# A pool for the score tiles that closes early, and the second stage's first weights decoded in it

## The chip, the cores and the metric

The kernel runs on one core of a Trainium2 chip. The metric is the device time of one execution in microseconds (us), as the median of several runs. Each core has a matrix engine (TensorE, in the rows PE, its weight loads PEld), three engines that work element by element (VectorE, DVE; ScalarE, ACT; GpSimd, POOL) and a queue that issues transfers (SyncE, SP). ACT issues transfers too, which then stand in its own queue (ACTq). Each engine works through its own instructions in the order of the program and waits, where it must, for a semaphore of another.

## The reference

Three parts follow each other. A recurrence over 768 steps for 4 x 8 heads of width 48, then two expert layers over the 3072 tokens of width 384:

```
cur   = (u * k_t) outer v_t
y_t   = r_t . (state + cur)
state = w_t * state + k_t outer v_t                      # 768 steps

x1 = (sigmoid(y @ w_gate) * (y @ w_val)) @ w_out         # 384 -> 1536 -> 384
h  = x1 @ w_in                                           # 384 -> 2048
out = (h * tanh(softplus(h))) @ w_out2                   # 2048 -> 384
```

## The kernel before

**Blocks.** Tokens are taken in 12 blocks of 64 steps for all batches, which are 256 tokens. For each block the recurrence runs in two steps of 32 (`step(j)`, 24 of them). Inside a block, the scores of eight steps and below are computed by POOL products (`pt`, from the block `blk` of r, k and w) and DVE sums into the tile `A`; larger distances go through PE (`lp`), and both are merged into `X`. PE makes the rows `yp`, ACT and DVE split them into two f16 halves `xs` (`split`, lines 202 and 205), and from block 2 on two transposing transfers that ACT issues (`send`, line 712) put them into `xt`, which the gates read. The state `s` is decayed (`decay`, line 754, on POOL or DVE) and joined with PE's outer products `kp` (line 792).

**First layer.** For block p, `gate(p, f)` with f = 0 to 11 makes two groups of 9 matmuls into one of four PSUM banks (`gv`, line 826), ACT takes the sigmoid (line 837), DVE multiplies (842), ACT and DVE write the f16 halves `gt` (854 and 857). `out1(p - 1, c, part)` runs beside it: for each of three columns c four groups of 9 matmuls into the single bank `po` (line 890), then ACT and DVE split the result into `xo` (202 and 205) and SP stores it. The next column's first group needs the bank back, and so the DVE half of `xo`.

**Second layer.** `h_unit` (PE at line 1006, weights `wis`) and `out2` (line 1051, weights `wps`) begin behind the last gate. Their 16 matmul groups per 512 tokens keep PE to the end.

**Weights.** All weights arrive as 64-bit numbers and are decoded in chunks to two f16 halves: `load_raw` (SP, 768 KB into a place `raw0` to `raw4`), on ACT `rebase` into `word` and `bits3` into `low`, on DVE `join` (line 273) and `sign` (284), then `high`, the cast (295, ACT or DVE), and `rest`, the subtraction (298, POOL or DVE). There are two `word` and two `low` places. `wi` has eight chunks and `wp` eight.

**Memory.** The recurrence's tiles lie in one pool `ap` on the right. `open_b` closes it when every task of the recurrence is done, and opens pools for `wis`, `wps`, two more `raw` places, two PSUM banks and the second layer's tiles in its room. So `high` and `rest` of `wi` and `wp` wait for `open`.

**Order.** The kernel does not write its order by hand: every piece is a task with an engine, an assumed cost, what it reads and what it writes, and `Plan.run` lays the tasks out in time by these costs and latest dates. The instructions are then issued in that order on each engine. A task that may run on two engines is put where it is planned first.

Of the kernel before, what the change touches and what calls it, by code (L numbers as in the profile page):

```python
# [7 lines left out]
F32 = mybir.dt.float32  # L8
F16 = mybir.dt.float16
# [7 lines left out]
DH = D // 2  # L17
# [6 lines left out]
BLK = C * (DH + DP + DH)  # L24
DM = H * D
KC = DM // 128
F1 = 1536
F2 = 2048
# [9 lines left out]
NPT = 32  # L38
NRAW = 2
# [8 lines left out]
W2HI = {"act": 0.83, "dve": 0.7}  # L48
W2LO = {"pool": 1.65, "dve": 0.92}
# [102 lines left out]
def mixer_moe_kernel(  # L152
# [23 lines left out]
    pg = ctx.enter_context(tc.tile_pool(name="pg", bufs=1, space=PS))  # L176
    po = ctx.enter_context(tc.tile_pool(name="po", bufs=1, space=PS))
    sa = ExitStack()
    sb = ExitStack()
    ap = sa.enter_context(tc.tile_pool(name="ap", bufs=1, side="right"))  # L180
    pp = sa.enter_context(tc.tile_pool(name="pp", bufs=1, space=PS, side="right"))

    x2d = dram.tile([NP, KC, 128, 2, NT], F16, name="x2d")
# [1 line left out]
    wgs = w1p.tile([128, 2, KC, F1], F16, name="wgs")  # L185
    wvs = w1p.tile([128, 2, KC, F1], F16, name="wvs")
    wos = w1p.tile([128, 2, NF1, DM], F16, name="wos")
    A = ap.tile([128, 1184], F32, name="A")
    KT = ap.tile([128, 2, BH, DP], F32, name="KT")
    U = ap.tile([128, DH], F32, name="U")  # L190
    mask = ap.tile([128, 2, C], F32, name="mask")
# [21 lines left out]
    def in_cols(w, s):  # L213
        v = w.bitcast(U32).rearrange("(c p) (f t) -> p c f t", p=128, t=2)
        return v[:, :, s]

    def in_rows(w, s):
        v = w.bitcast(U32).rearrange("(k p) (d t) -> p k d t", p=128, t=2)
        return v[:, s]
# [20 lines left out]
    def decode(key, dst, n, count, slot, reads, high_on, lo_on):  # L240
# [58 lines left out]
                out=dst()[:, 1], in0=words.pop(key), in1=dst()[:, 0], op=ALU.subtract  # L299
            )  # L300

        full = 1.55 if count < 6 else 0.95
        add("act", 0.9, rebase, [raw, "consts", "table1"], [word])
        add("act", 1.0, bits3, [raw, "consts"], [low])
        add("dve", full, join, [low], [word])
# [84 lines left out]
    blk = {}  # L390
# [21 lines left out]
    def load_pair(p):  # L412
        edges = (0, C * DH, C * (DH + DP), BLK)

        def new(e):
            blk[p] = ap.tile([128, BLK], F32, tag=f"blk{p % 2}", name=f"blk{p}")

        def go(e, i):
            if i is None:
                new(e)  # L420
            cs = slice(0, BLK) if i is None else slice(edges[i], edges[i + 1])
            nc.sync.dma_start(out=blk[p][:, cs], in_=rkw[p, :, cs])

        keys = [("blk", p % 2, i) for i in range(3)]
        if p:
            attn("sp", 3.6, lambda e: go(e, None), [], keys, lat=2.0)
        else:
            attn("none", 0, new, [], keys, lat=0.0)
            for i in range(3):
                attn("sp", 1.2, lambda e, i=i: go(e, i), [], [keys[i]], lat=2.0)  # L430
# [24 lines left out]
    def fine(p):  # L455
# [4 lines left out]
        def products(mult, cost, shape, cell, scaled=False):  # L460
            n = npt[0]
            npt[0] += 1
            pt = ("pt", n % 5)

            def go(e):
                pts[n] = ap.tile([128, NPT * DH], F32, tag=f"pt{n % 5}", name="pt")
                mult(e, shape(pts[n]), *rows(p)[:2])

            def times_u(e):
                u = U.unsqueeze(1).to_broadcast([128, C, DH])  # L470
                times(e, shape(pts[n]), shape(pts[n]), u)

            def total(e):
                nc.vector.tensor_reduce(  # L474
                    out=cell(), in_=shape(pts.pop(n)), op=ALU.add, axis=AX.X
                )

            attn("pool", cost * slow, go, [R, K], [pt])
            if scaled:
                attn("dve", 1.55, times_u, ["U"], [pt])  # L480
            cells.append(("A", len(cells)))
            attn("dve", 0.89 if cost > 1 else 0.5, total, [pt, "A"], [cells[-1]])

# [457 lines left out]
    nph = [0]  # L941
    nout = [0]

    def open_b(e):
        sa.close()
        w2["p"] = sb.enter_context(tc.tile_pool(name="w2p", bufs=1, side="right"))
        w2["raw"] = sb.enter_context(tc.tile_pool(name="raw", bufs=1, side="right"))
        w2["ph"] = sb.enter_context(tc.tile_pool(name="ph", bufs=1, space=PS, side="right"))
        w2["po"] = sb.enter_context(tc.tile_pool(name="po2", bufs=1, space=PS, side="right"))
        w2["wi"] = w2["p"].tile([128, 2, KC, F2], F16, name="wis")  # L950
        w2["wp"] = w2["p"].tile([128, 2, NF2, DM], F16, name="wps")
        w2["h"] = sb.enter_context(tc.tile_pool(name="hp", bufs=1, side="right"))

# [193 lines left out]
            load_pair(p + 2)  # L1147

    def tail_end():
        add("none", 0, open_b, [], ["attention", "open"])  # L1150
        chunks2 = []
        for i in range(8):
            cs = slice(256 * i, 256 * i + 256)
            dst = lambda cs=cs: w2["wi"][:, :, :, cs]
            chunks2.append((("wi", i), dst, in_cols(wi, cs), (KC, 256)))
        for i in range(8):
            cs = slice(2 * i, 2 * i + 2)
            dst = lambda cs=cs: w2["wp"][:, :, cs]
            chunks2.append((("wp", i), dst, in_rows(wo2, cs), (2, DM)))
        for i, (key, dst, src, n) in enumerate(chunks2):  # L1160
            slot = i % (3 + NRAW)
            pool = (lambda: dp) if slot < 3 else (lambda: w2["raw"])
            load_raw(key, pool, src, n, slot, [] if slot < 3 else ["open"])
            decode(key, dst, n, 6 + i, slot, ["open"], W2HI, W2LO)

    cells = {0: fine(0)}
    attn("pool", 2.0, masks, [], ["mask"])
# [84 lines left out]
```

## Time and profile before

| | before |
|---|---|
| median of 3 runs | 1033.44 us |
| lowest and highest | 1027.68 and 1035.75 us |
| profiled execution | 1026.83 us, span 1025.1 us |
| busy in the span: PE, DVE, ACT, POOL | 941.4, 527.4, 339.0, 311.8 us |
| mean granted TensorE clock | 0.990 |

The page of the profile shows one execution. Times in its rows are counted from the start of the span. "Idle" in a row is the time that the engine stood before that instruction, and the arrow names what ended it. The next-to-last section has the rows that the prediction reads.

### The profile page before, as it was taken

To read this page: it belongs to the slowest core of one execution; us is meant where nothing else is said; L and a number is where in the kernel's file an instruction comes from. 1 tells how busy PE (TensorE), PEld (TensorE's weight loads), DVE (VectorE), ACT (ScalarE), POOL (GpSimd) and SP (SyncE) were. 2 spreads that over 40 slices of the span, in tenths; PEclk is the share of its full clock that TensorE was granted. 3 is DMA by queue.
4 is the path that set the end of the run, shared out by engine and by line. 5 is a ranking of instruction groups with operands and counts; after the bars stand their busy time and mean duration, and the time that the engine had idled before them with its cause. 6 is when DMAs were issued, how large, how long until landed. Compare 5 with 4: busy or idle time off the path is not lost.

```text
span 1025.1 us, 32796 instructions
## 1 busy us (share of the span) xinstructions
PE 941.4 (92%) x14952; PEld 679.2 (66%) x14952; DVE 527.4 (51%) x840; ACT 339.0 (33%) x682; POOL 311.8 (30%) x324
## 2 busy tenths in 40 slices
PE   0287799989999999999999987999999999999998
PEld 0276678878878787878888876655555555555555
DVE  4899988866666656565554399721111111111110
ACT  3247622222222222222222255743333333333320
POOL 8872598771744545362010034100000000000000
PEclk9999899999999999999999999999999999999999
DMA  9355632333140304040210185010100101000000
GB/s 299 119 177 167 204 93 79 70 112 91 32 90 28 100 18 111 9 111 14 53 37 21 24 256 165 12 36 16 32 23 16 39 16 47 9 16 16 8 16 31
DMA packets 53595, 72.12 MB, mean 70 GB/s; under 512 B 20432, under 2 KB 37328, under 8 KB 52048
## 3 DMA queue, kind: packets, MB, share of 16 engines
q1 hardware_dynamic: 36816, 66.09, 20.9%
q10 hardware_dynamic: 16640, 3.94, 2.3%
q8 instruction: 117, 1.92, 0.8%
q14 instruction: 22, 0.18, 0.1%
HBM read 56.64 MB, written 9.44 MB: 64 GB/s over the span
## 4 chain that ended last, share of the span: by engine, by line
PE 79%; DVE 10%; DMA 3%; issue 2%; POOL 2%; ACT 2%; ACTq 0%; SPq 0%; DVEq 0%
PE gv L826 22%; PE o L1051 18%; PE h L1006 18%; PE o L890 12%; PE yp L678 3%; PE kp L781 3%; PE lp L593 3%; DMA raw_wo<-wo 1%; DVE A L474 1%; DVE word_wi L273 1%; POOL pt L453 1%; POOL blk L453 1%; DVE X L609 1%; DMA raw_wv<-wv 1%; DVE word_wi L284 1%
## 5 line engine op out<-in xcount | busy, mean ns | idle before, releaser
L1006 PE MATMUL h<-x,wis 128*128 128x512 f16 x864 | 201.5, 379 | 0.0
L890 PE MATMUL o<-gt,wos 128*128 128x256 f16 x1296 | 168.0, 275 | 12.1 <-DVE xo L205 9.6
L826 PE MATMUL gv<-xt,wgs 128*128 128x256 f16 x1296 | 167.6, 278 | 6.6 <-DVE gt L857 3.3
L826 PE MATMUL gv<-xt,wvs 128*128 128x256 f16 x1296 | 167.4, 275 | 3.0 <-issue 3.0
L890 PEld LDWEIGHTS <-wos 128*128 128x128 f16 x1296 | 127.4, 99 | 32.0 <-issue 12.3
L453 POOL TENSOR_TENSOR blk<-blk 128x384 f32<-128x384 f32 (+1 forms) x144 | 126.4, 895 | 71.1 <-DVE KD L564 59.4
L1006 PEld LDWEIGHTS <-wis 128*128 128x128 f16 x864 | 84.5, 98 | 90.8
L826 PEld LDWEIGHTS <-wgs 128*128 128x128 f16 x1296 | 125.2, 99 | 25.3 <-issue 7.3
L826 PEld LDWEIGHTS <-wvs 128*128 128x128 f16 x1296 | 121.5, 99 | 21.8 <-issue 3.3
L837 ACT ACTIVATE sig<-gv 128x256 f32<-128x256 f32 x144 | 55.1, 383 | 241.3 <-PE gv L826 238.0
L1017 ACT ACTIVATE e<-h 128x512 f32<-128x512 f32 x96 | 57.0, 597 | 197.8 <-PE h L1006 196.5
L453 POOL TENSOR_TENSOR pt<-blk 128x384 f32<-128x384 f32 (+1 forms) x96 | 107.4, 1144 | 42.4 <-DMA blk<-rkw 38.2
L842 DVE SCALAR_TENSOR_TENSOR gv<-gv,sig 128x256 f32<-128x256 f32 x144 | 61.7, 428 | 83.3 <-ACT sig L837 82.6
L854 ACT CAST gt<-gv 128x256 f16<-128x256 f32 x144 | 53.3, 372 | 80.7 <-DVE gv L842 70.1
L857 DVE TENSOR_TENSOR gt<-gv,gt 128x256 f16<-128x256 f32 x144 | 60.2, 419 | 35.2 <-ACT gt L854 35.2
L593 PE MATMUL lp<-RD,KD 64*16 64x16 f32 (+1 forms) x3072 | 34.5, 184 | 39.4 <-DVE RD L558 35.4
L1024 DVE SCALAR_TENSOR_TENSOR wos<-e,wos 128x512 f16<-128x512 f32 x27 | 18.7, 692 | 84.5 <-ACT wos L1020 84.5
L593 PEld LDWEIGHTS lp<-RD,KD 64*16 64x16 f32 (+1 forms) x3072 | 29.8, 101 | 48.5 <-DVE RD L558 35.4
L1051 PE MATMUL o<-wps,wgs 128*128 128x384 f16 x324 | 58.5, 326 | 0.0
L1051 PE MATMUL o<-wps,wos 128*128 128x384 f16 x324 | 57.2, 326 | 0.0
L474 DVE TENSOR_REDUCE A<-pt 128x32 f32<-128x768 f32 (+1 forms) x60 | 51.1, 863 | 4.2 <-POOL pt L453 4.2
L781 PE MATMUL kp<-v,KT 32*32 32x48 f32 x2944 | 44.9, 210 | 7.7 <-issue 6.7
(92 smaller groups left out, 1030.7 us busy)
## 6 DMA issues: line engine op xcount, KB each, us to landing
blk<-rkw SPq DMA_DIRECT2D x11, 1280.0 KB, 6.0
v<-vt SPq DMA_DIRECT2D x96, 96.0 KB, 3.3
raw_wi<-wi SPq DMA_DIRECT2D x8, 768.0 KB, 5.3
raw_wp<-wo SPq DMA_DIRECT2D x8, 768.0 KB, 4.5
raw_wg<-wg SPq DMA_DIRECT2D x6, 768.0 KB, 4.8
raw_wv<-wv SPq DMA_DIRECT2D x6, 768.0 KB, 4.8
raw_wo<-wo SPq DMA_DIRECT2D x6, 768.0 KB, 4.6
x2d<-xo SPq DMA_DIRECT2D x36, 128.0 KB, 1.8
```

Of the source, the lines that this page charges most:

```text
L453: engines[e].tensor_tensor(out=pv, in0=a, in1=b, op=ALU.mult)
L474: nc.vector.tensor_reduce(out=cell(), in_=shape(pts.pop(n)), op=ALU.add, axis=AX.X)
L593: nc.tensor.matmul(out, kd[p][gs, x, :m], rhs, start=True, stop=True, skip_group_check=True)
L781: nc.tensor.matmul(kps[j, hf][o : o + 32, i, :], KT[o : o + 32, p % 2, HG * e + x, :], vs[j][o : o + 32, x, :], start=True, stop=True,)
L826: nc.tensor.matmul(gps[p, f][:, o], w[:, a, kc, fs], xt[p][:, c, kc, :], start=(n == 0), stop=(n == 3 * KC - 1),)
L837: nc.scalar.activation(out=sgs[p, f], in_=gps[p, f][:, 0], func=AF.Sigmoid, scale=1.0 / (SW * SX))
L842: nc.vector.scalar_tensor_tensor(out=gps[p, f][:, 1], in0=gps[p, f][:, 1], scalar=SG / (SW * SX), in1=sgs.pop((p, f)), op0=ALU.mult, op1=A ...
L857: nc.vector.tensor_tensor(out=gt[p][:, 1, f], in0=gps[p, f][:, 1], in1=gt[p][:, 0, f], op=ALU.subtract,)
L890: nc.tensor.matmul(ops[p, c][:, :NT], wos[:, a, f, cs], gt[p][:, g, f, :], start=(f == 0 and n == 0), stop=(f == NF1 - 1 and n == 2),)
L1006: nc.tensor.matmul(hps[r, f], w2["wi"][:, a, kc, fs], x2[r][:, c, kc, :], start=(n == 0), stop=(n == 3 * KC - 1),)
L1017: nc.scalar.activation(out=es[r, f], in_=hps[r, f], func=AF.Mish, scale=ih)
L1051: nc.tensor.matmul(ops2[r, t][:, :DM], g2[r][f][:, c, tsl], w2["wp"][:, a, f, :], start=(f == 0 and n == 0), stop=(f == NF2 - 1 and n == 2),)
```

## The change

The tiles that only the scores inside eight steps use, which are `A`, the blocks `blk` and the products `pt`, move to a pool `fp` of their own. A new task `open_a` closes it when the tasks that use these tiles are done, which is before the recurrence ends, and opens a pool for `wis` in that room. The `wi` chunks now use three `raw` places that exist from the start, and their cast and subtraction wait for `opened` instead of `open`; the `wp` chunks still wait for `open`. The assumed cost of a join or sign is tied to the name `wo` instead of the chunk's number, which leaves the number for `wi` as it was (0.95).

```diff
+    sf = ExitStack()
     ap = sa.enter_context(tc.tile_pool(name="ap", bufs=1, side="right"))
+    fp = sf.enter_context(tc.tile_pool(name="fp", bufs=1, side="right"))
...
-    A = ap.tile([128, 1184], F32, name="A")
+    A = fp.tile([128, 1184], F32, name="A")
...
-        full = 1.55 if count < 6 else 0.95
+        full = 1.55 if key[0] == "wo" else 0.95
...
-            blk[p] = ap.tile([128, BLK], F32, tag=f"blk{p % 2}", name=f"blk{p}")
+            blk[p] = fp.tile([128, BLK], F32, tag=f"blk{p % 2}", name=f"blk{p}")
...
-                pts[n] = ap.tile([128, NPT * DH], F32, tag=f"pt{n % 5}", name="pt")
+                pts[n] = fp.tile([128, NPT * DH], F32, tag=f"pt{n % 5}", name="pt")
...
+    def open_a(e):
+
+        sf.close()
+        w2["i"] = sb.enter_context(tc.tile_pool(name="w2i", bufs=1))
+        w2["wi"] = w2["i"].tile([128, 2, KC, F2], F16, name="wis")
+
     def open_b(e):
         sa.close()
...
-        w2["wi"] = w2["p"].tile([128, 2, KC, F2], F16, name="wis")
         w2["wp"] = w2["p"].tile([128, 2, NF2, DM], F16, name="wps")
...
     def tail_end():
-        add("none", 0, open_b, [], ["attention", "open"])
-        chunks2 = []
+        done = [("blk", i, n) for i in range(2) for n in range(3)]
+        done += [("pt", i) for i in range(5)] + [("A", i) for i in range(8)] + ["A"]
+        add("none", 0, open_a, [], [*done, "opened"])
         for i in range(8):
             cs = slice(256 * i, 256 * i + 256)
             dst = lambda cs=cs: w2["wi"][:, :, :, cs]
-            chunks2.append((("wi", i), dst, in_cols(wi, cs), (KC, 256)))
+            load_raw(("wi", i), lambda: dp, in_cols(wi, cs), (KC, 256), i % 3)
+            decode(("wi", i), dst, (KC, 256), i, i % 3, ["opened"], W2HI, W2LO)
+        add("none", 0, open_b, [], ["attention", "open"])
         for i in range(8):
             cs = slice(2 * i, 2 * i + 2)
             dst = lambda cs=cs: w2["wp"][:, :, cs]
-            chunks2.append((("wp", i), dst, in_rows(wo2, cs), (2, DM)))
-        for i, (key, dst, src, n) in enumerate(chunks2):
-            slot = i % (3 + NRAW)
+            slot = (i + 2) % (3 + NRAW)
             pool = (lambda: dp) if slot < 3 else (lambda: w2["raw"])
-            load_raw(key, pool, src, n, slot, [] if slot < 3 else ["open"])
-            decode(key, dst, n, 6 + i, slot, ["open"], W2HI, W2LO)
+            reads = [] if slot < 3 else ["open"]
+            load_raw(("wp", i), pool, in_rows(wo2, cs), (2, DM), slot, reads)
+            decode(("wp", i), dst, (2, DM), i, slot, ["open"], W2HI, W2LO)
```

What the planner makes of it shows in the order of instructions. PE's order does not change. First ACT, from the rows `xs21` (step 21, the second half of block 10) to the evacuation of block 8's third column, `o18_2`. The first number behind `gv` and `gt` is the block. Before:

```order
L202 ACTIVATE xs21_9480<-yp21_9381 128x384
L712 DMA_TRANSPOSE xt10_9313<-xs21_9480 128x3x128 x2
L837 ACTIVATE sig_9549<-gv9_10_9470 128x256
L854 CAST gt9_8818<-gv9_10_9470 128x256
L837 ACTIVATE sig_9607<-gv9_11_9539 128x256
L854 CAST gt9_8818<-gv9_11_9539 128x256
L202 ACTIVATE xo_9621<-o18_2_9367 128x256
```

The same piece of ACT's order in the changed kernel:

```order
L204 ACTIVATE xs21_9504<-yp21_9396 128x384
L856 CAST gt9_8823<-gv9_9_9306 128x256
L297 CAST wis_9321<-word_wi3_9431 128x3x256
L714 DMA_TRANSPOSE xt10_9359<-xs21_9504 128x3x128 x2
L255 ACTIVATE word_wi4_9560<-raw_wi4_3349 128x768
L265 ACTIVATE low_wi5_9572<-raw_wi5_9458,floor3_87 128x768
L839 ACTIVATE sig_9586<-gv9_10_9493 128x256
L255 ACTIVATE word_wi5_9588<-raw_wi5_9458 128x768
L856 CAST gt9_8823<-gv9_10_9493 128x256
L265 ACTIVATE low_wi6_9635<-raw_wi6_9521,floor3_87 128x768
L839 ACTIVATE sig_9650<-gv9_11_9574 128x256
L297 CAST wis_9321<-word_wi4_9560 128x3x256
```

A gate's cast and the cast of `wi3` now stand between the rows and their sends, and `word` and `low` of the next chunks between the sends and the next sigmoid; two more casts of `wis` and `xo` come behind them.

Second DVE, from the first half of state 22 to the same `xo`. Before:

```order
L792 TENSOR_TENSOR s22_9299<-kp21_0_9495,s22_9299 128x384
L754 TENSOR_TENSOR s23_9482<-s22_9299,WD11_8526 128x384
L842 SCALAR_TENSOR_TENSOR gv9_10_9470<-gv9_10_9470,sig_9549 128x256
L857 TENSOR_TENSOR gt9_8818<-gv9_10_9470,gt9_8818 128x256
L792 TENSOR_TENSOR s22_9299<-kp21_1_9553,s22_9299 128x384
L754 TENSOR_TENSOR s23_9482<-s22_9299,WD11_8526 128x384
L842 SCALAR_TENSOR_TENSOR gv9_11_9539<-gv9_11_9539,sig_9607 128x256
L857 TENSOR_TENSOR gt9_8818<-gv9_11_9539,gt9_8818 128x256
L205 SCALAR_TENSOR_TENSOR xo_9621<-o18_2_9367,xo_9621 128x256
```

The same piece of DVE's order in the changed kernel:

```order
L794 TENSOR_TENSOR s22_9304<-kp21_0_9524,s22_9304 128x384
L275 SCALAR_TENSOR_TENSOR word_wi4_9560<-word_wi4_9560,low_wi4_9443 128x768
L844 SCALAR_TENSOR_TENSOR gv9_10_9493<-gv9_10_9493,sig_9586 128x256
L286 SCALAR_TENSOR_TENSOR word_wi4_9560<-raw_wi4_3349,word_wi4_9560 128x768
L859 TENSOR_TENSOR gt9_8823<-gv9_10_9493,gt9_8823 128x256
L794 TENSOR_TENSOR s22_9304<-kp21_1_9590,s22_9304 128x384
L275 SCALAR_TENSOR_TENSOR word_wi5_9588<-word_wi5_9588,low_wi5_9572 128x768
L844 SCALAR_TENSOR_TENSOR gv9_11_9574<-gv9_11_9574,sig_9650 128x256
L286 SCALAR_TENSOR_TENSOR word_wi5_9588<-raw_wi5_9458,word_wi5_9588 128x768
L207 SCALAR_TENSOR_TENSOR xo_9666<-o18_2_9380,xo_9666 128x256
```

The two decays of state 23 have gone to POOL, and a join and a sign for each of `wi4` and `wi5` stand around the gates, two of them right ahead of `xo`. Ahead of these rows, behind gate 7 of block 9, two joins, two signs, a cast and two subtractions of `wi1` to `wi3` are new.

## Rows read from the trace of the kernel before

**Rows 1.** The page's 40 equal slices, busy tenths: PE and DVE.

```profile
PE   0287799989999999999999987999999999999998
DVE  4899988866666656565554399721111111111110
```

**Rows 2.** Stretches: start:end, length, busy us of PE, PEld, DVE, ACT, POOL; clock, DMA.

```profile
531.00:547.00 16.00, 16.00 (x427) 13.54 (x426) 7.89 (x18) 3.80 (x10) 0.00 (x0) 1.00 0.25 60
547.00:558.00 11.00, 11.00 (x103) 9.78 (x100) 3.41 (x9) 2.65 (x7) 0.00 (x0) 1.00 0.04 13
558.00:586.00 28.00, 28.00 (x821) 23.67 (x820) 11.35 (x24) 6.55 (x17) 0.86 (x1) 1.00 0.08 20
586.00:636.00 50.00, 41.41 (x365) 36.04 (x363) 46.07 (x57) 27.64 (x49) 17.63 (x10) 0.97 0.66 205
```

**Rows 3.** PE in order of time: start, length, instructions, idle before and its end.

```profile
593.65 1.14 PE L890 MATMUL o<-gt,wos 128*128 128x256 f16 x9 [2.38 <-DVE xo L205]
...
608.62 1.14 PE L890 MATMUL o<-gt,wos 128*128 128x256 f16 x9 [1.05 <-DVE xo L205]
...
623.76 2.08 PE L890 MATMUL o<-gt,wos 128*128 128x256 f16 x9 [5.16 <-DVE xo L205]
625.63 1.67 PE L826 MATMUL gv<-xt,wvs 128*128 128x256 f16 x9
```

**Rows 4.** The stretch behind the longest wait; the granted clock is third from the end.

```profile
623.00:627.00 4.00, 3.24 (x17) 2.30 (x17) 3.94 (x8) 2.32 (x4) 1.22 (x1) 0.57 0.46 130
```

**Rows 5.** Groups by line, 586 to 636 us: count, busy us, mean ns, idle before.

```profile
L298 POOL TENSOR_TENSOR wis<-word_wi,wis 128x768 f16<-128x768 f32 x7 | 12.8, 1826 | 47.2 <-ACT xo L202 28.3 <-DVE wis L295 19.0
...
L273 DVE SCALAR_TENSOR_TENSOR word_wi<-word_wi,low_wi 128x768 uint32<-128x768 uint32 x6 | 9.7, 1616 | 0.3 <-ACT word_wi L253 0.3
L273 DVE SCALAR_TENSOR_TENSOR word_wp<-word_wp,low_wp 128x768 uint32<-128x768 uint32 x4 | 8.7, 2174 | 0.1
L284 DVE SCALAR_TENSOR_TENSOR word_wi<-raw_wi,word_wi 128x768 uint32<-128x768 uint32 x6 | 7.6, 1264 | 0.0
...
L842 DVE SCALAR_TENSOR_TENSOR gv<-gv,sig 128x256 f32<-128x256 f32 x12 | 5.0, 420 | 3.3 <-ACT sig L837 3.3
L857 DVE TENSOR_TENSOR gt<-gv,gt 128x256 f16<-128x256 f32 x12 | 5.0, 413 | 0.1
L298 POOL TENSOR_TENSOR wps<-word_wp,wps 128x768 f16<-128x768 f32 x3 | 4.9, 1639 | 8.6 <-DVE wps L295 8.6
```

**Rows 6.** DVE in order of time: a cast, two joins and a subtraction.

```profile
589.72 0.95 DVE L295 CAST wis<-word_wi 128x768 f16<-128x768 f32 x1 [0.53 <-DMA xt<-xs]
...
597.62 2.30 DVE L273 SCALAR_TENSOR_TENSOR word_wi<-word_wi,low_wi 128x768 uint32<-128x768 uint32 x1
...
607.28 0.94 DVE L273 SCALAR_TENSOR_TENSOR word_wi<-word_wi,low_wi 128x768 uint32<-128x768 uint32 x1
...
646.24 0.96 DVE L298 TENSOR_TENSOR wps<-word_wp,wps 128x768 f16<-128x768 f32 x1
```

**Rows 7.** POOL in order of time: a decay, and a subtraction.

```profile
530.00 0.83 POOL L754 TENSOR_TENSOR s<-s,WD 128x384 f32<-128x384 f32 x1 [2.85 <-PE yp L678]
...
597.45 1.65 POOL L298 TENSOR_TENSOR wis<-word_wi,wis 128x768 f16<-128x768 f32 x1 [5.01 <-DVE wis L295]
```

**Rows 8.** The page's DMA issues: count, KB each, median us to landing.

```profile
raw_wp<-wo SPq DMA_DIRECT2D x8, 768.0 KB, 4.5
```

**Rows 9.** PE in order of time: block 10's first gates, and a column's first group.

```profile
546.22 2.13 PE L826 MATMUL gv<-xt,wgs 128*128 128x256 f16 x18
...
549.17 1.15 PE L890 MATMUL o<-gt,wos 128*128 128x256 f16 x9
```

**Rows 10.** Groups by line, 531 to 558 us: the decays on DVE.

```profile
L754 DVE TENSOR_TENSOR s<-s,WD 128x384 f32<-128x384 f32 x3 | 1.7, 559 | 0.1
```

**Rows 11.** ACT's queue in order of time: the second pair of sends for block 10.

```profile
539.13 2.52 ACTq L712 DMA_TRANSPOSE xt<-xs  x2
```

**Rows 12.** The tile `xt`, 500 to 600 us: time of its transfers to landing.

```profile
DMA to landing us min/median/max: 2.3/2.9/4.1
```

## Prediction

> **What bounds the kernel now.** I start with the widest view, the 40 slices of the page: TensorE (PE) stands at 9 tenths from slice 8 on, except for slices 23 and 24 (575 to 625 us) with 8 and 7; in these VectorE (DVE) stands at 9, while it is at 5 or 6 ahead of them and at 1 behind [rows 1]. So PE is the bound, but for one place where DVE is. The table by stretch makes that exact: from 586 to 636 us PE is busy 41.41 of 50 us and DVE 46.07; from 531 to 586 PE is busy all the time, and DVE only 7.89 of 16, 3.41 of 11 and 11.35 of 28 us [rows 2]. Behind 636 us PE never waits.
>
> PE's order of time shows what fills the 8.6 us that PE lacks: three waits of 2.38, 1.05 and 5.16 us, each ended by DVE's `xo` at L205, the second half of the evacuation of the one bank `po` [rows 3]. And behind the longest, two groups of nine matmuls take 2.08 and 1.67 us instead of 1.14, another 1.47 us [rows 3]; the granted clock is 0.57 from 623 to 627 us [rows 4], so a part of these ran at the lower of the two levels, 1.2 GHz, after PE had stood for 5 us. Together this stretch loses 8.59 + 1.47 = **10.1 us**, and its PE work is 40 us. The groups by line say what DVE does there: joins and signs of `word_wi` and `word_wp` (9.7 + 8.7 + 7.6 us, and casts) against 5.0 + 5.0 us for the gates' own `gv` and `gt`, and three `xo` of the same shape at 0.41 [rows 5].
>
> **The change part by part.** No arithmetic goes away and PE's order stays, so the gain can only come from PE's waits, and 10.1 us is all there is. What is left of the eight `wi` chunks leaves this stretch for the last third of block 9 (531 to 558 us), and the bits of `wp0` go with it.
>
> *What the old stretch keeps.* On DVE: 11.2 us of `gv`, `gt` and `xo` [rows 5]; seven joins and seven signs of `wp` at 0.95 where nothing meets them (the row of 0.94 [rows 6]), 13.3; two casts of at most 0.95 and four subtractions at 0.96 [rows 6], 5.7: 30.2 us. To this comes POOL. A join takes 0.94 us alone, but 2.30 when a subtraction of 1.65 on POOL began 0.17 us ahead of it [rows 6, 7]. The ten joins and six `wi` signs of the stretch took 26.0 us, for 15.2 alone; that is 10.8 us of waiting for POOL's ten subtractions (seven `wis`, three `wps`), **1.1 us each** [rows 5]. The Trainium skill, "SBUF — State Buffer", section "Who interferes with whom", has a rule for this: a VectorE instruction with two SBUF inputs and a GpSimd instruction that reads SBUF exclude each other, and the later one waits for the whole of the earlier. The trace agrees: 2.30 is 0.94 and most of 1.65.
>
> In the new order four subtractions stay on POOL here: 30.2 + 4.4 = 34.6 us of DVE beside 40 of PE. It fits, where 46.07 did not. What remains are single waits. The first `wps` cast stands on ACT ahead of `xo`, and has to wait until attention's tiles are free, as the first `wis` cast did (589.72, released by the sends [rows 6]); a cast, `xo` on ACT, a subtraction and `xo` on DVE end near 591.9, where PE wants the bank at 591.1 (it got it at 593.6): 0.8 us. Then ACT stands at `low_wp1`, whose 768 KB can be asked for only now and land 4.5 us later [rows 8]; the gates behind it have four banks, and should take that. I take **1.5 us**, between 0.8 and 6 (that load, and one more `xo` late by it).
>
> *What the new stretch pays.* PE waits for nothing here today. The tight place is `xo` of block 8's third column: PE wants the bank at 549.17 [rows 9]. In the new DVE order there stand ahead of it, from 531 on, one cast of `wi` (0.95), two subtractions (0.96 each), four joins and four signs (8 x 0.95), less three decays of 0.56 [rows 10] that go to POOL: +8.8 us on the 7.89 that DVE works from 531 to 547 [rows 2], 16.7 us in the 18.2 to 549.17. So it just fits without meetings. But POOL has the subtractions of `wi0`, `wi2` and `wi4` at the same time, 3 x 1.1 = 3.3 us: 20.0, or 1.8 us too much. (Its three decays I count at nothing: most fall beside state joins that read PSUM.) And ACT is not free either: a pair of sends holds its queue 2.52 us [rows 11], and in the order shown `word_wi4` and the next sigmoid come behind the second pair, so that DVE stands some 1 us for its join. Sum for the new stretch **2.8 us**; bounds 0 (no meeting, no pause) and 8.4 (rival 2). What DVE owes at 558 (`wi7`, `wp0`) it works off by 586, with 16 us free there [rows 2].
>
> *The recurrence.* The second pair of sends now stands behind two casts; it was issued at 539.13 [rows 11], and PE's first gate of block 10 wants it at 546.22 [rows 9]. The sign of `wi3` meets POOL, its cast follows at 540.9, the pair is issued from 541.7 and the second of it lands 2.9 us (2.3 to 4.1 [rows 12]) after about 542.9: 545.8, just in time. I count nothing; at 4.1 it costs 0.8 us, within the bounds above.
>
> *SP and the early order.* All `wi` loads now use the three `raw` places that exist from the start, each issued when the sign three chunks back is done, ahead of column stores that nobody waits for soon. The first `x2` loads fall some 3 us later, and PE needs them at 636: 40 us of cover. In blocks 1 to 3 a join, a sign, one `low_wi3` and one POOL product change places, hidden by the pauses of engines that PE does not wait for there. Nothing, with bounds of ±2 us.
>
> **Sum.** -10.1 + 1.5 + 2.8 = -5.8 us. The profiled execution took 1026.83 us (span 1025.1); it becomes 1021.0. The median of the runs shown is 1033.44, 6.6 us more, in a spread of 8 us; so I forecast the median at **1027.6 us**.
>
> **Rivals.** *1. All is regained.* DVE has 15.7 us free from 531 to 558, and the new order puts joins into the pauses between a gate's `gv` and `gt`. For it: 16.7 in 18.2 us. Against it: 1.1 us for each meeting. Then only the 0.8 us stays: -9.3, 1024.1 at the median (1017.5 from the profiled execution).
>
> *2. Meetings at full length.* Place: DVE from 531 to 549, ahead of `xo`. Three subtractions of 1.64 and three decays of 0.83 [rows 7] are waited for in full, 7.4 us, and DVE stands for one whole pair of sends, 2.5: 16.7 + 7.4 + 2.5 - 18.2 = 8.4 us. With the same beside `wps`, 3 us in the old stretch: -10.1 + 11.4 = +1.3, 1034.7 at the median, not faster. It decides from 7 us in the new stretch on. For it: the four joins of `wp` took 2.17 us on the mean [rows 5]. Against it: the signs of `wi` took 1.26, so most met nothing. The page's rule above would make each meeting as dear as this.
>
> *3. The old stretch hardly gets better*, since `wps` still waits for attention and its loads then hold ACT: 6 us there and 2.8 in the new, -1.3, 1032.1. For it: the first of the three waits came before much had been decoded.
>
> That the change does nothing is excluded: on ACT the first casts of `wis` now stand ahead of sends without which attention cannot end, so they cannot wait for its end.
>
> **How the numbers follow.** Forecast 0.50 (its own range 1024.5 to 1031), rival 1 0.15, rival 2 0.17, rival 3 0.15, the rest to the early order. The range for 8 in 10 reaches from rival 1 in a low run to rival 2 with 2 us more: 1017 to 1036.8. One per cent, about what a measurement of this kernel can tell from no change, is 10.3 us. Faster by more needs rival 1 and a low run, 0.12; slower by more needs 20 us of new stops, 0.04; within it 0.84.
>
> **What would show it.** In the profile after: PE busy nearly all of 586 to 636 us, no wait over 2 us there and the granted clock at 1.00; a new wait of PE `o` for DVE `xo` near 549 us, of 2 to 4 us (none: rival 1; 7 or more: rival 2); joins of `word_wi` at 1.3 to 1.7 us on the mean; DVE at 8 or 9 tenths in slices 21 and 22. I am wrong if PE waits for the sends (`xt`) in block 10, or for `wis` at the start of the second stage, or if its waits ahead of 500 us change by more than 2 us.

## The result, and the profile after

| | before | after |
|---|---|---|
| median, in runs side by side (20 each) | 1032.21 us | 1022.28 us |
| lowest and highest | 1024.20 and 1037.93 us | 1016.55 and 1030.89 us |
| ratio of after to before | | 0.9913, 95% interval 0.9892 to 0.9934 |
| profiled execution | 1026.83 us, span 1025.1 us | 1025.36 us, span 1023.6 us |
| busy in the span: PE, DVE, ACT, POOL | 941.4, 527.4, 339.0, 311.8 us | 941.2, 512.9, 347.1, 307.6 us |

The change takes 9.0 us off (0.0087 x 1032.2; interval 6.8 to 11.1 us). The forecast was 5.8 us, and 1027.6 us for the median.

The 40 slices of the page after, against [rows 1]:

```profile
PE   0388789989999899989999999999999999999998
DVE  5899988866666556666658557221111111111110
```

Slices are counted from 0. DVE's two slices at 9 (23 and 24, 589 to 641 us) now have 5 and 7, slice 21 (537 to 563 us) has risen from 4 to 8, and PE is at 9 in slices 23 and 24. The stretches of [rows 2] after, columns as there:

```profile
531.00:547.00 16.00, 16.00 (x481) 13.43 (x481) 12.77 (x19) 8.63 (x17) 7.45 (x7) 1.00 0.34 98
547.00:558.00 11.00, 9.64 (x160) 8.08 (x149) 8.60 (x14) 7.03 (x13) 4.62 (x3) 1.00 0.64 175
558.00:586.00 28.00, 27.46 (x662) 23.25 (x663) 18.61 (x32) 12.29 (x26) 2.51 (x2) 1.00 0.39 128
586.00:636.00 50.00, 49.50 (x614) 43.05 (x603) 33.63 (x57) 29.73 (x57) 7.23 (x4) 1.00 0.37 113
```

From 586 to 636 us PE is busy 49.50 instead of 41.41 us, DVE 33.63 instead of 46.07, and the clock is 1.00 instead of 0.97. But a stretch of fixed times does not hold the same work in two traces: at 586 us the trace after is some 8 us behind in PE's order. The PE instructions that run from 586.08 to 636.19 us before (DVE busy 46.26 us there) run from 594.25 to 634.70 us after:

```profile
594.25:634.70 40.45, 39.95 (x365) 35.38 (x363) 30.37 (x50) 26.49 (x50) 7.23 (x4) 1.00 0.44 133
```

From 547 to 558 us PE lacks 1.36 us that it did not lack before. Its waits of more than 0.25 us from 531 us on are these three, in order of time:

```profile
553.46 2.12 PE L828 MATMUL gv<-xt,wgs 128*128 128x256 f16 x18 [1.28 <-DVE gt L859]
...
567.95 1.14 PE L892 MATMUL o<-gt,wos 128*128 128x256 f16 x9 [0.54 <-DVE xo L207]
...
623.68 1.14 PE L892 MATMUL o<-gt,wos 128*128 128x256 f16 x9 [0.29 <-DVE xo L207]
```

The three waits and the slow groups of [rows 3] have become one wait of 0.29 us. In the new stretch PE waits 1.28 us at the first gate of block 10 and, ahead of block 9's second column, 0.54 us for `xo` of its first. The first row names DVE's `gt`, but that ended just then by chance: in four of the kernels below the row of the same wait names `DMA xt<-xs`. What the gate waits for are the sends, as the ACT queue, POOL and DVE ahead of it show, in order of time:

```profile
544.00 1.64 POOL L300 TENSOR_TENSOR wis<-word_wi,wis 128x768 f16<-128x768 f32 x1 [3.26 <-ACT wis L297]
...
544.17 2.28 DVE L286 SCALAR_TENSOR_TENSOR word_wi<-raw_wi,word_wi 128x768 uint32<-128x768 uint32 x1
546.37 0.55 DVE L207 SCALAR_TENSOR_TENSOR xs<-yp,xs 128x384 f16<-128x384 f32 x1
...
546.54 3.10 ACTq L714 DMA_TRANSPOSE xt<-xs  x2
```

The tile `xt` from 544 to 556 us, the two transfers of this pair:

```profile
DMA to landing us min/median/max: 5.3/6.0/6.8
```

The first was issued at 546.54 and the longest took 6.8 us: 553.34, and the gate starts at 553.46. In the profile before, the same pair took 2.3 to 2.4 us.

### The profile page after: what moved, and what is told of

Its sections match the earlier page's. It is cut to its first block, busy times and chain, and to the rows that moved or that the text cites. A ratio compares the mean times of both kernels' runs of the same rounds, so it can differ in the third digit from the quotient of the medians.

```text
span 1023.6 us, 32777 instructions
## 1 busy us (share of the span) xinstructions
PE 941.2 (92%) x14952; PEld 678.8 (66%) x14952; DVE 512.9 (50%) x831; ACT 347.1 (34%) x693; POOL 307.6 (30%) x322
## 4 chain that ended last, share of the span: by engine, by line
PE 78%; DVE 9%; DMA 4%; issue 3%; POOL 2%; ACT 2%; ACTq 0%; SPq 0%; DVEq 0%
PE gv L828 22%; PE o L1058 18%; PE h L1013 18%; PE o L892 11%; PE yp L680 3%; PE kp L783 3%; PE lp L595 3%; DMA raw_wo<-wo 1%; POOL pt L455 1%; DVE A L476 1%; POOL blk L455 1%; DVE word_wi L286 1%; DMA raw_wp<-wo 1%; DMA raw_wv<-wv 1%; DVE X L611 1%
## 5 line engine op out<-in xcount | busy, mean ns | idle before, releaser
L1031 DVE SCALAR_TENSOR_TENSOR wgs<-e,wgs 128x512 f16<-128x512 f32 x27 | 18.7, 692 | 73.8 <-ACT wgs L1027 73.8
```

## The experiments

For each kernel the table gives the change of time over the same PE instructions, from that which starts at 531.0 us in the trace before to that which starts at 700.0 us there (the start of the second minus the start of the first, less 169.0); PE's waits of over 0.25 us in it; and the ratio to the kernel before with its 95% interval. The kernels tried for this section that have a ratio were timed in five rounds; the three without had one execution.

| kernel | 531 to 700 us | PE's waits there, us | ratio |
|---|---|---|---|
| before | 0 | 2.38, 1.05, 5.16 | |
| b_again (before once more) | -0.03 | 2.08, 4.71 | 1.0018 (0.9992 to 1.0044) |
| changed kernel | -7.3 | 1.28, 0.54, 0.29 | 0.9913 (0.9892 to 0.9934) |
| e1_late | -1.4 | 1.87, 4.91 | 0.9945 (0.9915 to 0.9975) |
| e1_again | -0.7 | 1.62, 4.91 | 0.9967 (0.9942 to 0.9991) |
| e2_half | -7.2 | 1.07, 1.63 | 0.9933 (0.9905 to 0.9961) |
| e5_dve | -8.4 | 1.22 | 0.9913 (0.9877 to 0.9948) |
| e6_pool | -7.6 | 0.71, 0.92, 0.42 | 0.9910 (0.9880 to 0.9939) |
| e3_sent | -7.6 | 0.92, 1.51 | |
| e4_loads | -7.2 | 1.05, 1.33 | |
| e4_held | -0.8 | 0.40, 6.20 | |
| e9_holdsent | -8.1 | 1.36 | 0.9902 (0.9866 to 0.9938) |
| e10_pace | -9.1 | 0.39 | 0.9875 (0.9845 to 0.9906) |
| e11_dvepace | -9.3 | none (0.24 at most) | 0.9844 (0.9816 to 0.9872) |

**The kernel before, once more.** No edit.

> The kernel before, unchanged, as a kernel of its own: a second profile of it and a ratio of equals. If the three waits for xo from 586 to 636 us belong to the order of work, they come back within 0.5 us each (8.6 us in all, then two slow groups), and the time over the same PE instructions from 531 to 700 us differs by under 0.5 us from the first profile. The ratio is 1.000 with an interval of about 0.003; PE's waits ahead of 531 us that no engine ended (4 to 8 us from 200 to 250 us and from 300 to 375 us) may move by several us.

Its waits for `xo` in order of time:

```profile
599.75 2.06 PE L890 MATMUL o<-gt,wos 128*128 128x256 f16 x9 [2.08 <-DVE xo L205]
...
629.87 1.48 PE L890 MATMUL o<-gt,wos 128*128 128x256 f16 x9 [4.71 <-DVE xo L205]
```

Two of the three waits come back; the second, of 1.05 us, does not, and instead the group behind the first takes 2.06 us where 1.14 is usual, and the clock from 586 to 636 us is 0.93. The time over the stretch is the same to 0.03 us. So the 10.1 us belong to the order of work, though not to three waits of fixed length.

**Undoing the early decode.** Pools, raw places and the code of the loads stay; `wi` is decoded as late as before, and so the loads that need a raw place back go out later too (none from 420 to 590 us):

```diff
+        add("none", 0, open_b, [], ["attention", "open"])
         for i in range(8):
...
-            decode(("wi", i), dst, (KC, 256), i, i % 3, ["opened"], W2HI, W2LO)
-        add("none", 0, open_b, [], ["attention", "open"])
+            decode(("wi", i), dst, (KC, 256), i, i % 3, ["open"], W2HI, W2LO)
```

> The pools and the raw places stay as in the changed kernel, but cast and subtraction of all eight wi chunks wait for the recurrence's end again. Theory (the gain is only DVE work that leaves the stretch from 586 to 636 us): PE's waits for xo of 8 to 11 us come back there, the granted clock dips behind the longest, and the ratio to the kernel before is 0.997 to 1.003. Rival (the new places of the tiles, the raw places or the order of loads save time themselves): the ratio stays near 0.991 and PE waits under 2 us in that stretch.

The waits for `xo` are back, 6.78 us of them where I expected 8 to 11, and no more than 1.4 us of the stretch is saved. But the ratio, 0.9945, is below what I expected of it. So I ran it again:

> The kernel of e1_late once more, since its ratio (0.9945) said 2.6 to 8.8 us less and its trace only 1.4 us less over the same PE instructions from 531 to 700 us. If its trace is right and the early decode is the gain, the ratio comes out at 0.996 to 1.001 and the second profile again at 0 to 3 us less. If the raw places and the order of loads give some 4 us by themselves, it is 0.993 to 0.996 again, and the second profile shows it either from 531 to 700 us or ahead of it.

```profile
593.47 1.14 PE L892 MATMUL o<-gt,wos 128*128 128x256 f16 x9 [1.62 <-DVE xo L207]
...
622.12 2.08 PE L892 MATMUL o<-gt,wos 128*128 128x256 f16 x9 [4.91 <-DVE xo L207]
```

Again the same two waits, and 0.9967, with an interval (0.9942 to 0.9991) that reaches into both of its theories. Both traces say that eight to nine tenths of what the changed kernel saves from 531 to 700 us hang on the early decode. The ratios of the two leave 3 to 6 us of gain, of which the traces show 1: what the rest is, I take up below.

**Half of the dose.** `wi0` to `wi3` wait for `opened`, `wi4` to `wi7` for `open`:

```diff
+        part(0, 4, "opened")
         add("none", 0, open_b, [], ["attention", "open"])
+        part(4, 8, "open")
```

`part` is the loop of the changed kernel over some of the chunks, with the task that they wait for.

> wi0 to wi3 are decoded early, wi4 to wi7 wait for the recurrence's end. Theory A (each chunk that leaves gives its share, about 1.2 us of the 9.6): PE waits 3 to 6 us in the old stretch, ratio 0.994 to 0.997. Theory B (a threshold: PE waits only where DVE's work in the stretch comes near PE's): with 33.6 us of DVE work plus at most 8 the stretch of 50 us still holds it, PE waits under 2 us there and under 1 us in the new stretch, ratio 0.988 to 0.992.

Half of the chunks give 7.2 of the 7.3 us, with one wait of 1.63 us left in the old stretch (theory B, but for 1.07 us at block 10's first gate). From the matmul at 586.1 us on, ahead of which the new stretch lies, it is 8.7 of 9.7 us. The interval of the ratio holds both theories, so the trace decides here: PE's waits are not in proportion to the work removed. Over the PE instructions from 586.08 to 636.19 us before, DVE is busy 36.13 us here beside PE's 39.79, and that is nearly hidden, where 46.26 us were not (45.60 in b_again).

**DVE and POOL.** All eight subtractions of `wi` on DVE, and all on POOL:

```diff
-            decode(("wi", i), dst, (KC, 256), i, i % 3, ["opened"], W2HI, W2LO)
+            decode(("wi", i), dst, (KC, 256), i, i % 3, ["opened"], W2HI, {"dve": 0.92})
```

```diff
-            decode(("wi", i), dst, (KC, 256), i, i % 3, ["opened"], W2HI, W2LO)
+            decode(("wi", i), dst, (KC, 256), i, i % 3, ["opened"], W2HI, {"pool": 1.65})
```

> All eight subtractions of wi on DVE, none on POOL, so that no decode on DVE meets one in the early stretch. If the forecast's price holds (1.1 us for a meeting), signs of wi fall from a mean of 1.42 to 0.95 us from 531 to 586 us and subtractions from 1.07 to 0.96, 3.3 us in all, while four more subtractions cost 3.8 us: PE's waits move by less than 1 us, ratio 0.989 to 0.993. If POOL's subtractions were what makes PE wait at block 10's first gate (the sign of wi3 took 2.28 us ahead of the sends), this wait of 1.28 us goes below 0.3.

> All eight subtractions of wi on POOL. At 1.1 us a meeting DVE gains 3.8 us and loses about as much again as in the changed kernel, 4 to 5 us: no more than 1 us on PE, ratio 0.989 to 0.994. If the meetings were the bound of the new stretch (rival 2), PE's waits from 531 to 586 us grow from 1.8 to 4 us or more and the ratio goes to 0.994 or above.

Signs, joins and subtractions of `wi` on DVE from 531 to 586 us, groups by line with count, busy time and mean ns. The changed kernel:

```profile
L286 DVE SCALAR_TENSOR_TENSOR word_wi<-raw_wi,word_wi 128x768 uint32<-128x768 uint32 x6 | 8.5, 1420 | 0.0
...
L275 DVE SCALAR_TENSOR_TENSOR word_wi<-word_wi,low_wi 128x768 uint32<-128x768 uint32 x6 | 5.7, 953 | 2.4 <-ACT word_wi L255 2.4
L300 DVE TENSOR_TENSOR wis<-word_wi,wis 128x768 f16<-128x768 f32 x4 | 4.3, 1071 | 0.9 <-ACT wis L297 0.8
```

e5_dve, in which none of them meets a subtraction of `wi` on POOL:

```profile
L275 DVE SCALAR_TENSOR_TENSOR word_wi<-word_wi,low_wi 128x768 uint32<-128x768 uint32 x6 | 5.9, 1004 | 0.2
L286 DVE SCALAR_TENSOR_TENSOR word_wi<-raw_wi,word_wi 128x768 uint32<-128x768 uint32 x6 | 5.7, 948 | 0.0
```

e6_pool, with eight subtractions on POOL:

```profile
L286 DVE SCALAR_TENSOR_TENSOR word_wi<-raw_wi,word_wi 128x768 uint32<-128x768 uint32 x6 | 6.7, 1113 | 0.0
L275 DVE SCALAR_TENSOR_TENSOR word_wi<-word_wi,low_wi 128x768 uint32<-128x768 uint32 x6 | 6.2, 1030 | 3.7 <-ACT word_wi L255 3.7
...
L275 DVE SCALAR_TENSOR_TENSOR word_wp<-word_wp,low_wp 128x768 uint32<-128x768 uint32 x1 | 1.4, 1423 | 0.4 <-ACT word_wp L255 0.4
```

The meetings of the changed kernel cost 6 x 0.47 + 4 x 0.12 = 3.3 us of DVE; without them signs take 0.95. The forecast had 3.3 us too, but for three subtractions ahead of `xo` of block 8's third column. Ahead of that `xo` only two signs are longer, 2.28 and 1.25 us: 1.6 us. The other 1.7 come behind it, and a fourth subtraction has a part in them. With eight subtractions on POOL they cost less, not more (6 x 0.16 + 6 x 0.08 + 0.47 for the join of `wp0` = 1.9 us), since fewer fall together. PE's time over the stretch is 1.1 and 0.3 us shorter than in the changed kernel, so the meetings are not what bounds it, and rival 2 is out. And the wait at block 10's first gate stays at 1.22 us in e5_dve, where no meeting delays the sign of `wi3`; so the meeting ahead of the sends is not its cause:

```profile
549.29 1.91 PE L828 MATMUL gv<-xt,wgs 128*128 128x256 f16 x16 [1.22 <-DMA xt<-xs]
```

**The sends of block 10.** Three runs set apart their issue and their landing. First the sign and the cast of `wi3` behind the sends, then the loads of `raw_wi5` and `raw_wi6` behind their landing:

```diff
-        add("dve", full, sign, [raw], [word])
+        add("dve", full, sign, [raw, *sent], [word])
...
+            sent = [("xt", 0, 1, x) for x in range(2)] if i == 3 else []
```

> Sign and cast of wi3 stand behind the second pair of sends of block 10. Theory S (the sends are issued late): the pair is issued 0.7 to 1.0 us behind the last row yp, instead of 2.3, and PE's wait at block 10's first gate (1.28 us) falls below 0.3 although the transfers still need 5 to 7 us to land. Theory L (they land late because loads of raw_wi move at the same time): the issue is as early, the landing is not, and a wait of 0.3 us or more stays if the landing is above 6 us.

```diff
+            hold = [("xt", 0, 1, x) for x in range(2)] if i in (5, 6) else []
-            load_raw(("wi", i), lambda: dp, in_cols(wi, cs), (KC, 256), i % 3)
+            load_raw(("wi", i), lambda: dp, in_cols(wi, cs), (KC, 256), i % 3, hold)
```

> The loads of raw_wi5 and raw_wi6 wait until the sends of block 10 have landed; the decode's order ahead of the sends stays, so they are issued 2.3 us behind the last row yp as in the changed kernel. Theory L: transfers of xt land in 2.3 to 3.5 us instead of 5 to 6.8, and PE waits under 0.3 us at block 10's first gate. Theory S: the landing still takes over 4.5 us and the wait stays at 0.8 to 1.3 us. The held loads move the decode of wi5 to wi7 some 5 us later, which has 28 us of room.

This one did not do what it says: what a task reads sets its place in the planned order, but the instruction waits only for data that it touches, and SP had nothing to wait for. The loads went out 1.2 us ahead of the last row `yp` and 2.2 us behind it, as in the changed kernel; it is a second look at that kernel. So the loads were held by data:

```diff
+            if hold is not None:
+                nc.gpsimd.tensor_copy(
+                    out=raws[key].bitcast(F32)[:, 0, 0:2, 0:1], in_=xt[hold][:, :, 0, 255:256]
+                )
             nc.sync.dma_start(out=raws[key], in_=src)
...
+            load_raw(("wi", i), lambda: dp, in_cols(wi, cs), (KC, 256), i % 3, hold, 10 if hold else None)
```

> In the run e4_loads the loads went out all the same (at 544.0 and 547.4 us), since what a task reads sets only its place in the planned order. Here they are held in fact: POOL copies two numbers of xt of block 10 into the raw place, and the load of raw_wi5 and raw_wi6 follows that copy. The decode's order ahead of the sends stays. Theory L (the transfers of xt land late because loads of raw_wi move beside them): they land in 2.3 to 3.2 us instead of 5.1 to 6.8, and PE waits under 0.3 us at block 10's first gate although the pair is issued 2.3 us behind the last row yp. Rival: they land in over 4.5 us with no load beside them, and PE waits 0.8 to 1.3 us. wi5 to wi7 are decoded some 6 us later, which may bring a wait for xo of up to 2 us from 558 to 586 us.

Times below are counted from the end of the last row `yp` of step 21, in each trace; "loads beside" are 768 KB loads of `raw_wi` issued from 2 us ahead of that end to the second send.

| kernel | first and second send issued | loads beside | landing, us | wait at block 10's first gate |
|---|---|---|---|---|
| before | 0.6, 1.9 | 0 | 2.3 to 2.4 | none |
| b_again | 0.6, 2.1 | 0 | 2.4 to 2.5 | none |
| e1_late | 0.6, 2.2 | 0 | 2.4 to 2.7 | none |
| e1_again | 0.6, 1.9 | 0 | 2.3 to 2.4 | none |
| e4_held | 2.2, 3.5 | 0 | 3.6 to 4.4 | none |
| e3_sent | 0.6, 1.9 | 1 | 3.3 to 4.3 | none |
| e9_holdsent | 0.6, 1.9 | 1 | 3.8 to 4.8 | none |
| e10_pace | 0.6, 1.9 | 1 | 3.5 to 4.5 | none |
| e11_dvepace | 2.0, 3.2 | 1 | 3.8 to 4.8 | none |
| changed kernel | 2.2, 4.1 | 2 | 5.3 to 6.8 | 1.28 |
| e2_half | 2.2, 4.4 | 2 | 5.0 to 6.8 | 1.07 |
| e4_loads | 2.2, 3.7 | 2 | 5.1 to 5.5 | 1.05 |
| e5_dve | 2.1, 3.5 | 2 | 5.8 to 6.8 | 1.22 |
| e6_pool | 1.2, 3.2 | 2 | 5.5 to 7.2 | 0.71 |

ACT's queue in e3_sent, and PE's first wait:

```profile
553.39 3.15 ACTq L714 DMA_TRANSPOSE xt<-xs  x2
...
564.51 1.14 PE L892 MATMUL o<-gt,wos 128*128 128x256 f16 x9 [0.92 <-DVE xo L207]
```

ACT's queue and the tile `xt` of e4_held, from 547 to 562 us:

```profile
548.66 3.72 ACTq L718 DMA_TRANSPOSE xt<-xs  x2
...
DMA to landing us min/median/max: 3.6/4.0/4.4
```

PE's waits for `xo` in e4_held:

```profile
557.62 1.14 PE L896 MATMUL o<-gt,wos 128*128 128x256 f16 x9 [0.40 <-DVE xo L207]
...
574.59 2.08 PE L896 MATMUL o<-gt,wos 128*128 128x256 f16 x9 [6.20 <-DVE xo L207]
```

In five traces with two loads beside the sends these land in 5.0 to 7.2 us, in four with one in 3.3 to 4.8, in four of the five with none in 2.3 to 2.7; e11_dvepace lands like the others with one load, though its issue is as late as the changed kernel's. So theory L holds for the larger part: the transfers land late because loads move beside them. It is not all: e4_held, with the same late issue and no load, still needs 3.6 to 4.4 us, more than I expected. Traffic does not explain that: of 0.29 MB that moved there from 545 to 556 us, 0.20 are the sends' own. Its cause stays open. The gate loses its wait where the landing is shorter by 2 us, with the issue as late as ever (e4_held), and in e3_sent, where the issue comes 1.6 us earlier. Before, the gate starts 7.7 us behind the last row `yp`. In the changed kernel the first send lands 2.2 + 6.8 = 9.0 us behind it, which gives the wait; 0.6 + 6.8 would have been in time, an estimate from these rows. So it takes both, the late issue and the late landing, and the forecast had counted the first. But e3_sent does not isolate the issue, since the sign behind the sends also freed the raw place later and sent the second load away.

e3_sent shows a second thing. With the first gate on time, PE waits 0.92 us for `xo` of block 8's third column, and 1.51 for the next: nearly nothing is won over the stretch (-7.6 against -7.3). The 1.28 us at the gate had covered the first of them: in the changed kernel that `xo` ends at 556.59 us, 0.05 us ahead of PE's first matmul there (556.64), so without the gate's wait PE would have stood for it. And e4_held shows what a DVE that is late costs: its decode of `wi5` to `wi7` came 5 to 8 us later, DVE worked 14.87 of 17 us from 563 to 580, and PE waited 6.20 us, where I had expected up to 2, with the clock at 0.80 there:

```profile
563.00:580.00 17.00, 10.80 (x193) 8.42 (x191) 14.87 (x18) 8.70 (x16) 6.99 (x5) 0.80 0.58 194
```

**Both of these together.** The order of e3_sent with the holds of e4_loads, which set only the plan:

> Both: sign and cast of wi3 behind the sends, and the loads of raw_wi5 and raw_wi6 behind their landing. PE's wait at block 10's first gate is gone, the wait for xo near 568 us (0.54 us) may stay: over the same PE instructions from 531 to 700 us 8.5 to 9.5 us less than before, where the changed kernel has 7.3 less. The ratio is 0.987 to 0.992, too near to the changed kernel's 0.9913 to be told apart by time alone; the trace tells it.

One wait of 1.36 us for `xo` of block 8's third column is left, where the forecast had put the price of the new stretch. The first gate waits for nothing.

```profile
550.82 1.14 PE L892 MATMUL o<-gt,wos 128*128 128x256 f16 x9 [1.36 <-DVE xo L207]
```

**Pacing.** The joins of `wi4` to `wi7` are planned behind that `xo` as well; in the second kernel the subtractions of `wi` are all on DVE:

```diff
-        add("dve", full, join, [low], [word])
-        add("dve", full, sign, [raw], [word])
+        add("dve", full, join, [low, *after], [word])
+        add("dve", full, sign, [raw, *sent], [word])
...
+            sent = [("xt", 0, 1, x) for x in range(2)] if i == 3 else []
+            after = [("xo", 2, 1)] if i >= 4 else []
```

> Sign and cast of wi3 are planned behind the sends of block 10, and the joins of wi4 to wi7 behind xo of block 8's third column, so that nothing of the decode stands ahead of the two things PE wants from 540 to 560 us. If sends and this xo are all that PE waits for in the new stretch, its waits from 531 to 600 us fall from 1.8 to under 0.5 us, and over the same PE instructions from 531 to 700 us it needs 9 to 10 us less than before, where the changed kernel needs 7.3 less: ratio 0.986 to 0.991. Rival (DVE has too little room, so the wait only moves on): a wait of 1 to 3 us for the next xo, near 568 us or 580 us.

> The same, and all eight subtractions of wi on DVE, so that no join or sign meets one. DVE has 3.8 us more of its own work and some 3 us less of meetings: 9 to 10.5 us less than before over the same PE instructions, ratio 0.985 to 0.991. Rival as above; if subtractions on DVE are what makes the next xo late, its waits are longer than in e10_pace.

e11_dvepace in the stretches of [rows 2]:

```profile
531.00:547.00 16.00, 16.00 (x436) 13.51 (x425) 12.49 (x22) 10.05 (x17) 1.72 (x3) 1.00 0.42 111
547.00:558.00 11.00, 11.00 (x103) 9.85 (x102) 10.19 (x17) 8.04 (x15) 1.35 (x1) 1.00 0.66 203
558.00:586.00 28.00, 27.76 (x759) 23.36 (x758) 15.91 (x31) 10.59 (x23) 2.17 (x2) 1.00 0.37 114
586.00:636.00 50.00, 49.81 (x480) 41.08 (x478) 34.45 (x58) 33.08 (x61) 7.03 (x4) 1.00 0.36 110
```

PE is busy nearly throughout, with no wait above 0.24 us and none above 0.19 for `xo`. The rival of a moved wait does not come. Over the same PE instructions (those from 531 to 547, 547 to 558 and 558 to 586 us before) DVE works 12.24, 10.53 and 15.50 us, in the changed kernel 14.64, 10.28 and 14.60: there was room, but not ahead of what PE wanted next. The ratio is 0.9844, about 16 us; its interval and that of the changed kernel do not touch, though it overlaps that of e10_pace, and this kernel has the lowest median (1016.73 us). The trace accounts for 9.3 of the 16.

## Why the prediction was right, and where not

**What bounds the kernel: right.** The 10.1 us come back in a second profile of the kernel before to 0.03 us, and most of them in e1_late and e1_again.

**The old stretch keeps 1.5 us: too much.** DVE's work was put at 34.6 us; over the same PE instructions it is busy for 30.37, since its instructions overlap a little (their lengths add up to 33.2) and the four subtractions on POOL cost some 2.4 us instead of 4.4 (joins at a mean of 0.97, signs 1.14, subtractions 1.19 there). PE waits 0.29 us. From the matmul at 586.1 us before to that at 700.0 the changed kernel is 9.67 us shorter, so 0.4 us stay. Neither the cast of `wps` ahead of `xo` nor the load behind `low_wp1` made PE wait. Rival 3 is out.

**The new stretch pays 2.8 us: 2.4 measured, but not where I said.** PE was to wait for `xo` at 549 us. It waited 1.28 us at block 10's first gate, where I had counted nothing for the sends, 0.54 us for the next `xo`, and some 0.5 us lie in groups of matmuls that took longer. That 2.4 is near 2.8 is luck. The step that failed is the landing of 2.9 us, which measured 5.3 to 6.8. It came from a stretch in which no weights were loaded (DMA share 0.25 and 0.04 [rows 2]), while the change puts loads of 768 KB into just that stretch (0.34 and 0.64 after). The trace before had the right row a few blocks earlier, where the recurrence's blocks are loaded; the tile `xt` before, from 250 to 300 us:

```profile
DMA to landing us min/median/max: 3.0/5.9/8.5
```

The Trainium skill, "DMA: Bandwidth & Descriptors", section "Issuing engines are not separate DMA queues", says that transfers issued by different engines run on the same 16 DMA engines and interleave. The landings in the table above agree: sends from ACT's queue take 2.3 us alone and up to 7.2 beside two loads from SP's. The issue itself I had even put too late: 3.2 us behind the last row, and it was 2.2.

The mechanism that I did price is there too. As soon as the sends are on time, PE waits 0.92 (e3_sent) or 1.36 us (e9_holdsent) for that `xo`, a third to a half of the 2.8. It was hidden by the wait ahead of it.

**Meetings of DVE and POOL: right in kind, too dear in the forecast.** 3.3 us were forecast ahead of `xo` and 1.6 measured there; the 3.3 measured over the whole stretch agree by chance. They fell on the signs, at a mean of 1.42, not on the joins, which I had put at 1.3 to 1.7 and which took 0.95. One meeting can still be dear: 2.28 us for the sign of `wi3` when POOL's subtraction of 1.64 us had begun 0.17 us earlier. The Trainium skill, "SBUF — State Buffer", section "Who interferes with whom", lets the later of the two wait for the whole of the earlier; this row agrees (0.95 and 1.47 left of POOL's 1.64, less what overlaps at the start). The rival that made every meeting as dear fails on their number: e6_pool, with twice as many subtractions on POOL, pays 1.9 us for them.

**The sum.** Forecast -5.8 us, trace -7.3, by the ratio -9.0. The median came out 5.3 us below the forecast: 1.2 because the kernel before was at 1032.2 instead of 1033.4 us in the runs side by side, 1.5 from the two stretches, and 2.6 that the stretches don't show. The trace is nearer to the forecast, the ratio to rival 1 (-9.3); but rival 1's mechanism, no price in the new stretch, is what only e10_pace and e11_dvepace come near, with 0.5 and 0.7 us.

**The early order: open.** I counted nothing, within 2 us. In eight of the nine measured kernels with the new places and loads the ratio gives more than the trace, by 0.6 to 6.8 us (e1_late 4.2, e1_again 2.7, the changed kernel 1.7, e11_dvepace 6.8, e2_half -0.3). That looks like a gain ahead of 531 us that they share. But a single trace can't show it: in two profiles of the very same kernel before, the matmul at 531 us comes 6.4 us apart, and in e1_late and e1_again, which are the same kernel too, 10.2 us. Of these 10.2 a single stop at one instruction makes 7.1, first in e1_late, then in e1_again:

```profile
214.40 1.46 PE L828 MATMUL gv<-xt,wvs 128*128 128x256 f16 x6 [8.65 <-issue]
```

```profile
206.94 0.83 PE L828 MATMUL gv<-xt,wvs 128*128 128x256 f16 x6 [1.51 <-issue]
```

And each ratio by itself is uncertain by 2 to 4 us. Set the lowest run of each kernel against the lowest run of the kernel before in the same rounds, and in six of the nine the difference is within 0.7 us of the trace (the changed kernel -7.7 us against -7.3); e1_late, e10_pace and e11_dvepace have 2.0, 2.3 and 3.2 us more. So a good part of what the ratios show beyond the traces may be such stops. No run here isolates it.

My sign that waits ahead of 500 us must not change by more than 2 us was worthless for this reason; the other sign, a wait for the sends in block 10, came true: by it the prediction was wrong on how the price arises.

Two readings of the slices in the prediction are off. Slices 23 and 24 are 589 to 641 us, not 575 to 625, and DVE's digit ahead of them is 4 and 3, not 5 or 6; the sum does not rest on them. And of the slices 21 and 22, forecast at 8 or 9, the first has 8 and the second 5.

## What to carry to other kernels

Price a transfer by a row from a stretch with the traffic that the change will cause, not by the quiet stretch into which the change moves its loads. When work moves into free time of an engine, what counts is not whether it fits the stretch but what stands right ahead of the two or three instructions that the bound engine wants next; planning the moved work behind these (e11_dvepace) brought a price of 2.4 us down to 0.7. And a wait can cover another one: take it away alone (e3_sent) and the next appears.

## What I had not expected of the hardware

PE stops at the same instruction in every trace for a time that differs from run to run and that no engine ends ("issue"). The second matmul row of one gate group, in the kernel before, in its second profile, and after:

```profile
349.80 1.03 PE L826 MATMUL gv<-xt,wgs 128*128 128x256 f16 x8 [1.50 <-issue]
```

```profile
351.83 1.44 PE L826 MATMUL gv<-xt,wgs 128*128 128x256 f16 x6 [4.24 <-issue]
```

```profile
353.31 1.01 PE L828 MATMUL gv<-xt,wgs 128*128 128x256 f16 x4 [4.27 <-issue]
```

1.50 and 4.24 us for one kernel, at one place; three such places lie between 345 and 460 us, about 50 us apart, in each of the fourteen traces. In PE's order, with matmuls and weight loads counted together, they stand 2048 and 2304 instructions apart, both multiples of 256. Between the two profiles of the kernel before they make 4.3 of the 6.4 us that lie between them at 531 us. The runs of one kernel spread over 14 us, more than this change is worth; how much of that such stops make, and what ends them, was not tried.

The transposing sends of block 10 hold ACT's queue for different times too: 2.52 us for the pair in the kernel before [rows 11], 3.10 after and 3.15 in e3_sent. Loads beside them do not explain it: e4_held has 3.72 us with none, e5_dve 2.53 us with two.
